# Three sets of transposes moved from the matrix engine to transposing DMAs

## The chip, the cores and the metric

One Trainium2 chip, one core. The metric is the device time of one execution in microseconds (us); lower is better. The core has a matrix engine (PE, with its weight loads listed apart as PEld), a vector engine (DVE), a scalar engine (ACT), GpSimd (POOL) and a synchronising engine (SP) that issues most DMAs. Each engine works through its own list of instructions in order and waits on semaphores for the others.

## The reference

Two independent layers on inputs of 2048 tokens by 448 features, in bfloat16; their outputs are laid side by side.

```
# layer A: a diagonal complex state-space layer, 448 states
Lam_bar = exp(dt * Lam);  B_bar = ((Lam_bar - 1) / Lam)[:, None] * Bmat
Bu = x @ B_bar.T                       # (2048, 448), complex
h[t] = Lam_bar * h[t-1] + Bu[t]        # over 2048 steps
y = 2 * Re(h @ Cmat.T) + x * Dskip
# layer B: 16 heads of 28, each token looks at 8 keys, 2 apart, backwards
q, k, v = split(x @ wqkv)
logits = q . k[pos - 2w] * 28**-0.5,  w = 0..7;  softmax over w
o = sum_w attn[w] * v[pos - 2w];  out = o @ wo
```

## The kernel before

PE multiplies with the contracted axis on the partitions, so both inputs are needed with features on partitions, and so is the attention output `o` before it meets `wo`. Tokens are cut into 16 per partition (token 16p+j is partition p, column j) for the attention output and for layer A, and into four chunks of 512 for the logits. Features are cut 4 by 112. The stages, in program order:

- Loads (SP's queue): layer B's x in four pieces (`xb_sb`), the three parts of `wqkv` (`wqkv_nat`), layer A's `bX` and `cn`, `wo_p`, and later layer A's x (`xa_sb`), which shares its buffer with `xb_sb`.
- Start: PE warm-up matmuls, layer A's parameters (`pt_p`, `pt_d` and many small DVE and ACT operations), then chunk 0 of x transposed (`pt_x`, copied to `xbT`) and projected to kT and qT (`qk_ps`).
- Logit stage, `qk(c)` for four chunks: DVE forms 8 products of q with shifted k (`pr`), PE sums them over features (`lg`); between them PE does the next chunk's transposes and projections, then `setup_b` (`pt_b`, giving `Bcat`) and the v projection (`v_ps`). Each chunk ends in a maximum (`pt_m`, `mx`, `mxb`) and an exponential (`e_all`).
- `norm`: sums of exponentials by PE (`tp`), division by DVE (`rec`, `attn`).
- Value stage, `pv` in four calls of 4 columns: 15 DVE operations each over 128x1792 elements (`pvb`, `pvt`), 60 in all. Each call ends in `tail`: PE transposes `o` (`pt_o`), ACT copies it (`oT`), PE multiplies by `wo_p` (`wo_ps`), ACT copies (`yb`), SP stores.
- Beside it layer A: x transposed (`pt_x`, `xaT`), `local` (`u_ps`, ACT copies `u`) for four column phases b, `scan` over chunks of 16 tokens (`g3`, `rot`, `bak` on PE, `pc`, `psn`, `gsc` on DVE), `groups` (`gt` on PE, `Gt` on DVE), `correct` (`co`) for phases 1, 0 and 2, and `y` per column (`y_ps`, ACT copies `ya`, SP stores).

A scheduler sets each engine's order from the program's order and its own priorities; the order is fixed once built. Every DMA raises one of eight completion semaphores, used in turn, and an issue waits until the DMA that last used its semaphore has landed. PSUM tiles come from three pools by tag: "mm" (3 buffers), "pt" (2), "lg" (3).

Of the kernel before, what the change touches and what calls it, by code (L numbers as in the profile page):

```python
# [31 lines left out]
PL = 64  # L32
MA = 4
# [54 lines left out]
class PartB:  # L88
# [6 lines left out]
    def load_x(self, n0, n1):  # L95
        if n0 == 0:
            self.x_sb = self.pool.tile([NCH, T, D], bf16, name="xb_sb", tag="xin")
        xv = self.B_x[0].rearrange("(n p) d -> p n d", p=NCH)
        self.nc.sync.dma_start(self.x_sb[:, n0:n1, :], xv[:, n0:n1, :])

    def load_w(self, which):
        if which == 1:
            self.wn = self.pool.tile([KP, KT, 3, D], bf16, name="wqkv_nat", tag="wn")
        v = self.B_wqkv.rearrange("(k p) (w c) -> p k w c", p=KP, w=3)
        self.nc.sync.dma_start(self.wn[:, :, which, :], v[:, :, which, :])

    def load_wo(self):
        nc = self.nc
        self.wo_p = self.pool.tile([KP, KT, D], bf16, name="wo_p")
        wo_v = self.B_wo.rearrange("(h kt dl) c -> dl h kt c", kt=KT, dl=7)  # L110
        for dl in range(7):
            nc.sync.dma_start(self.wo_p[dl * H:(dl + 1) * H, :, :], wo_v[dl])

    def alloc(self):
        pool, nc = self.pool, self.nc
        self.xT = pool.tile([KP, KT, S], bf16, name="xbT", tag="xT")
# [35 lines left out]

    def transp(self, n, eng):
        nc, cx = self.nc, self.cx
        pt = cx.ps([KP, KT, 2, NCH], bf16, "pt_x", "pt")
        for i in range(2):
            for k in range(KT):
                nc.tensor.transpose(pt[:, k, i, :], self.x_sb[:, n + i, k * KP:(k + 1) * KP], cx.ident[:])
        cx.ev(eng, self.xT[:, :, n * NCH:(n + 2) * NCH], pt[:].rearrange("p k i c -> p k (i c)"))
# [76 lines left out]
    def pv(self, j0, j1):  # L236
# [16 lines left out]
        for j in range(j0, j1, 2):  # L253
            self.tail(j, acc[:, j - j0:j - j0 + 2])

    def tail(self, j, o_):
        nc, pool, cx = self.nc, self.pool, self.cx
        pt = cx.ps([KP, KT, 2, NCH], bf16, "pt_o", "pt")
        o_ = o_.rearrange("p j d h -> p j (d h)")
        for i in range(2):  # L260
# [3 lines left out]
        nc.scalar.copy(oT[:], pt[:])  # L264
        yb = pool.tile([NCH, 2, D], bf16, name="yb", tag="yb", bufs=2)
        for i in range(2):
            ps = cx.ps([NCH, D], f32, "wo_ps", "lg")
            for kt in range(KT):
                nc.tensor.matmul(ps[:], lhsT=oT[:, kt, i, :], rhs=self.wo_p[:, kt, :], start=(kt == 0),  # L269
                                 stop=(kt == KT - 1))  # L270
            nc.scalar.copy(yb[:, i, :], ps[:])  # L271
        nc.sync.dma_start(self.out_b[:, j:j + 2, :], yb[:])


class PartA:
# [7 lines left out]
    def load_params(self):  # L283
        nc, pool = self.nc, self.pool
        self.prow = pool.tile([3 * NM, 2, PL], bf16, name="prow")
        self.drow = pool.tile([KT, KP], bf16, name="drow")
# [16 lines left out]
    def load_x(self):  # L303
        self.x_sb = self.pool.tile([NCH, T, D], bf16, name="xa_sb", tag="xin")
        xv = self.A_x[0].rearrange("(p j) d -> p j d", j=T)
        for g in range(2):
            self.nc.sync.dma_start(self.x_sb[:, 8 * g:8 * g + 8, :], xv[:, 8 * g:8 * g + 8, :])
# [10 lines left out]
    def params(self):  # L318
# [79 lines left out]
    def params_g(self):  # L398
# [46 lines left out]
    def setup_b(self, engs):  # L445
        nc, cx, pool = self.nc, self.cx, self.pool
        self.Bcat = pool.tile([KP, KT, NM, NCH], bf16, name="Bcat")
        for i in range(NM):
            pt = cx.ps([KP, KT, NCH], f32, "pt_b", "pt")
            for k in range(KT):  # L450
                nc.tensor.matmul(pt[:, k, :], lhsT=self.bX[:, i, k * KP:(k + 1) * KP], rhs=self.mats["g"][:, i, :],
                                 start=(k == 0), stop=(k == KT - 1), skip_group_check=True)
            cx.ev(engs[i % len(engs)], self.Bcat[:, :, i, :], pt[:])
            yield
# [14 lines left out]
    def alloc(self):  # L469
        pool = self.pool  # L470
        xa = pool.tile([KP, 4, KT, 4, NCH], bf16, name="xaT", tag="xT")
        self.xT = {i: xa[:, i] for i in range(4)}
        u01 = pool.tile([NCH, 2, NM, 4 * NCH], bf16, name="u01", tag="q")
        self.h = [u01[:, 0], u01[:, 1], None, None]

    def transp(self, b, eng):
        nc, cx = self.nc, self.cx
        t_ = self.xT[b]
        for a in range(0, 4, 2):
            pt = cx.ps([KP, KT, 2, NCH], bf16, "pt_x", "pt")  # L480
            for i in range(2):
                for k in range(KT):
                    nc.tensor.transpose(pt[:, k, i, :], self.x_sb[:, 4 * (a + i) + b, k * KP:(k + 1) * KP],
                                        cx.ident[:])
            cx.ev(eng, t_[:, :, a:a + 2, :], pt[:])
            yield

    def local(self, b):
        nc, cx = self.nc, self.cx
        if b == 2:  # L490
            u23 = self.pool.tile([NCH, 2, NM, 4 * NCH], bf16, name="u23", tag="xin")
            self.h[2], self.h[3] = u23[:, 0], u23[:, 1]
        for m in range(NM):
            ps = cx.ps([NCH, 4 * NCH], f32, "u_ps", "mm")
            for k in range(KT):
                nc.tensor.matmul(ps[:], lhsT=self.Bcat[:, k, m, :], rhs=self.xT[b][:, k].rearrange("p a c -> p (a c)"),  # L496
                                 start=(k == 0), stop=(b % 2 == 0 and k == KT - 1))
            if b % 2:
                nc.tensor.matmul(ps[:], lhsT=self.mats[1][:, m, :], rhs=self.h[b - 1][:, m, :], start=False,
                                 stop=(b == 1))  # L500
            if b == 3:
                nc.tensor.matmul(ps[:], lhsT=self.mats[2][:, m, :], rhs=self.h[1][:, m, :], start=False, stop=True)  # L502
            nc.scalar.copy(self.h[b][:, m, :], ps[:])  # L503
# [7 lines left out]
    def scan(self):  # L511
# [6 lines left out]
        pc = [pool.tile(tab, bf16, name=f"pc{i}") for i in range(2)]  # L518
        psn = [pool.tile(tab, bf16, name=f"psn{i}") for i in range(2)]
        g = pool.tile(tab, f32, name="gsc")  # L520
# [78 lines left out]
    def y(self, a, b):  # L599
# [3 lines left out]
        for k in range(KT):  # L603
            nc.tensor.matmul(ps[:, k * KP:(k + 1) * KP], lhsT=self.xT[b][:, k, a, :], rhs=self.Dg[:, k, :],  # L604
# [10 lines left out]
def body(ctx: ExitStack, tc: tile.TileContext, A_x, A_Lre, A_Lim, A_Bre, A_Bim, A_Cre, A_Cim, A_logdt, A_Dskip,  # L615
# [54 lines left out]
    for _ in chain(transp(0), proj(0), transp(1)):  # L670
        pass
    weave(b.qk(0), chain(proj(1), transp(2)), 2)
    weave(b.qk(1), chain(proj(2), transp(3)), 2)
    a.params_g()
    weave(b.qk(2), chain(proj(3), a.setup_b("A")), 2)
    a.load_x()
# [4 lines left out]
    for _ in a.transp(0, "A"):  # L681
        pass
    weave(a.local(0), chain(a.transp(1, "A"), a.transp(2, "A")))
    weave(a.local(1), chain(a.transp(3, "A"), a.setup_c("A")))
    for b_ in (2, 3):
# [8 lines left out]
    for b_ in (1, 0, 2):  # L694
        for _ in a.correct(b_, "A"):
# [39 lines left out]
```

## Time and profile before

| | |
|---|---|
| Time, median of 2 runs | 178.68 us (177.88 to 179.47) |
| The profiled execution: time | 177.29 us |
| The profiled execution: span of the trace | 175.3 us |
| PE busy | 159.6 us |
| DVE busy | 132.6 us |
| ACT busy | 108.9 us |
| POOL busy | 5.6 us |

The profiled execution took 1.99 us more than its span, for what lies before the first and after the last traced instruction. Rows of the timeline read: start, length, engine, line, operation, output<-input, sizes, count, and in brackets how long the engine was idle before it and what ended that. SPq is SP's queue issuing DMAs.

### The profile page before, as it was taken

The page shows a single profiled execution, that of the slowest core. Times are in us where ns is not written, and L with a number is a line of the kernel's source. Part 1 is how long each engine was busy: PE and PEld are TensorE (multiplying, and loading weights), DVE is VectorE, ACT ScalarE, POOL GpSimd, SP SyncE. Part 2 cuts the span into 40 slices and gives each one's busy share as a digit, 9 for nine tenths or more (in the row PEclk, how much of TensorE's full clock was granted, in tenths as well). Part 3 has the DMA queues.
Part 4 walks back from the last instruction along what each step waited for, and adds up shares of the span by engine and source line. Part 5 has one row for each costly group of instructions (what it writes and reads, how often), then busy time and mean ns, then how long its engine had stood idle before and what let it go on. Part 6 is the DMA issues. An engine that isn't in the chain of part 4 may idle for free.

```text
span 175.3 us, 2965 instructions
## 1 busy us (share of the span) xinstructions
PE 159.6 (91%) x1171; PEld 90.8 (52%) x1175; DVE 132.6 (76%) x189; ACT 108.9 (62%) x183; POOL 5.6 (3%) x37
## 2 busy tenths in 40 slices
PE   7589798799799999999999999969999999999981
PEld 4355333445444766676565444746755455554550
DVE  1299998999996894039999999999999999900000
ACT  2279444775744876788899654356238739738382
POOL 8400000000000000000000000000000000000000
PEclk9999999999999999999999999999999999999999
DMA  5999851000370004170000000002111230140113
GB/s 155 291 297 179 90 119 30 0 4 0 87 332 0 6 0 109 50 200 8 0 4 0 0 0 0 4 0 77 33 52 52 79 108 26 52 132 30 52 54 105
DMA packets 16589, 12.36 MB, mean 70 GB/s; under 512 B 7219, under 2 KB 16065, under 8 KB 16575
## 3 DMA queue, kind: packets, MB, share of 16 engines
q1 hardware_dynamic: 16504, 12.16, 26.2%
q8 instruction: 9, 0.15, 0.4%
q14 instruction: 5, 0.04, 0.1%
q10 hardware_dynamic: 71, 0.01, 0.0%
HBM read 6.89 MB, written 3.67 MB: 60 GB/s over the span
## 4 chain that ended last, share of the span: by engine, by line
PE 51%; DVE 32%; ACT 10%; DMA 3%; issue 1%; ACTq 1%
PE y_ps L607 11%; PE qk_ps L165 11%; DVE pvb L252 9%; DVE pvt L249 8%; PE v_ps L177 7%; PE wo_ps L269 5%; PE lg L196 5%; DVE pr L192 4%; DMA drow<-in_A_Dskip_dram 3%; PE co L577 2%; ACT u L588 2%; DVE pvb L249 2%; PE y_ps L604 2%; ACT oT L264 2%; PE gt L566 1%
## 5 line engine op out<-in xcount | busy, mean ns | idle before, releaser
L192 DVE TENSOR_TENSOR pr<-qT,kT 112x2048 bf16<-112x2048 bf16 x32 | 37.0, 1219 | 0.5 <-ACT qT L77 0.5
L165 PE MATMUL qk_ps<-xbT,wqkv_nat 112*112 112x512 bf16 x128 | 32.3, 386 | 1.4 <-ACT xbT L77 1.1
L252 DVE TENSOR_TENSOR pvb<-pvb,pvt 128x1792 bf16<-128x1792 bf16 x28 | 30.3, 1083 | 0.0
L249 DVE TENSOR_TENSOR pvt<-attn,vd 128x1792 bf16<-128x1792 bf16 x28 | 30.0, 1083 | 0.0
L496 PE MATMUL u_ps<-xaT,Bcat 112*128 112x512 bf16 x112 | 27.4, 379 | 0.1
L503 ACT CAST u<-u_ps 128x512 bf16<-128x512 f32 x28 | 16.5, 590 | 9.2 <-PE u_ps L502 5.0
L165 PEld LDWEIGHTS <-wqkv_nat 112*112 112x112 bf16 x128 | 14.9, 129 | 14.1 <-issue 6.9
L607 PE MATMUL y_ps<-C,u 128*128 128x448 bf16 x84 | 18.0, 352 | 0.0
L610 ACT CAST ya<-y_ps 128x448 bf16<-128x448 f32 x16 | 8.5, 533 | 15.1 <-PE y_ps L607 14.2
L496 PEld LDWEIGHTS <-Bcat 112*128 112x128 bf16 x112 | 10.5, 97 | 10.8 <-issue 0.2
L269 PE MATMUL wo_ps<-wo_p,oT 112*128 112x448 bf16 x64 | 14.3, 353 | 1.0 <-ACT oT L264 0.9
L196 PE MATMUL lg<-pr,onesW 112*32 112x512 bf16 x128 | 12.8, 387 | 1.1 <-DVE pr L192 1.1
L177 PE MATMUL v_ps<-wqkv_nat,xbT 112*128 112x448 bf16 x64 | 13.7, 357 | 0.0
L77 ACT CAST kT<-qk_ps 112x512 bf16<-112x512 f32 x14 | 8.2, 584 | 8.1 <-PE qk_ps L165 8.1
L77 ACT CAST qT<-qk_ps 112x512 bf16<-112x512 f32 x14 | 8.2, 584 | 6.7 <-PE qk_ps L165 6.7
L271 ACT CAST yb<-wo_ps 128x448 bf16<-128x448 f32 x16 | 8.6, 539 | 5.8 <-PE wo_ps L269 5.6
L77 ACT CAST vd<-v_ps 128x448 bf16<-128x448 f32 x16 | 8.5, 533 | 4.5 <-PE v_ps L177 4.3
L177 PEld LDWEIGHTS <-xbT 112*128 112x128 bf16 x64 | 8.8, 146 | 4.0 <-issue 1.3
L210 DVE TENSOR_REDUCE mx<-pt_m 128x64 bf16<-128x512 bf16 x4 | 2.7, 687 | 10.5 <-PE pt_m L209 10.5
L588 ACT CAST u<-co 128x512 bf16<-128x512 f32 x21 | 10.6, 629 | 0.0
L607 PEld LDWEIGHTS <-u 128*128 128x128 bf16 x84 | 7.6, 97 | 5.5
L264 ACT COPY oT<-pt_o 112x1024 bf16<-112x1024 bf16 x8 | 8.1, 1047 | 2.5 <-PE pt_o L262 2.5
(175 smaller groups left out, 218.5 us busy)
## 6 DMA issues: line engine op xcount, KB each, us to landing
xb_sb<-in_B_x_dram SPq DMA_DIRECT2D x4, 448.0 KB, 7.0
xa_sb<-in_A_x_dram SPq DMA_DIRECT2D x2, 896.0 KB, 6.4
out_dram<-yb SPq DMA_DIRECT2D x8, 224.0 KB, 2.1
out_dram<-ya SPq DMA_DIRECT2D x16, 112.0 KB, 1.7
wqkv_nat<-in_B_wqkv_dram SPq DMA_DIRECT2D x3, 392.0 KB, 6.4
vd<-vd SPq DMA_DIRECT2D x1, 784.0 KB, 5.3
vd<-vd SPq DMA_DIRECT2D x1, 588.0 KB, 4.3
bX<-in_A_B_re_dram SPq DMA_DIRECT2D x1, 392.0 KB
```

Source lines behind the costliest of these rows:

```text
L77: nc.scalar.copy(out, in_)
L165: nc.tensor.matmul(ps[:], lhsT=self.wn[:, k, which, g * KP:(g + 1) * KP], rhs=self.xT[:, k, c * CH:(c + 1) * CH], start=(k == 0), stop=(k ...
L177: nc.tensor.matmul(ps[:], lhsT=xv[:, k, j, :], rhs=self.wn[:, k, 2, :], start=(k == 0), stop=(k == KT - 1))
L192: V.tensor_tensor(pr[:], self.qT[:, :, c * CH:(c + 1) * CH], self.kT[:, :, k0:k0 + CH], op=ALU.mult)
L196: nc.tensor.matmul(lg[NW * g:NW * (g + 1), :], lhsT=self.onesW[:, NW - 4 - 4 * w:2 * NW - 4 - 4 * w], rhs=pr[:, g, :], start=(w == 0), sto ...
L249: V.tensor_tensor(t_[:, 0:n], self.at[:, w, j0:j1, :].unsqueeze(2).to_broadcast([NCH, n, DH, H]), self.vd[:, off:off + n], op=ALU.mult)
L252: V.tensor_tensor(acc[:, 0:n], acc[:, 0:n], t_[:, 0:n], op=ALU.add)
L269: nc.tensor.matmul(ps[:], lhsT=oT[:, kt, i, :], rhs=self.wo_p[:, kt, :], start=(kt == 0), stop=(kt == KT - 1))
L496: nc.tensor.matmul(ps[:], lhsT=self.Bcat[:, k, m, :], rhs=self.xT[b][:, k].rearrange("p a c -> p (a c)"), start=(k == 0), stop=(b % 2 == 0 ...
L503: nc.scalar.copy(self.h[b][:, m, :], ps[:])
L588: nc.scalar.copy(h_, ps[:])
L607: nc.tensor.matmul(ps[:], lhsT=self.state(m, a, b), rhs=self.C[:, m, :], start=False, stop=(m == NM - 1), skip_group_check=True)
```

## The change

All 192 PE transposes named `pt_x` and `pt_o`, and the copies behind them, are gone. In their place stand 13 transposing DMAs on SP's queue.

- Layer B's x: each chunk of 512 tokens is written transposed into `xbT` by two DMAs from HBM, one for features 0 to 383 (three slabs of 128), one for features 320 to 447. `wqkv` is loaded in the same cut; the fourth slab's first 64 rows are zero (a memset on POOL), since those features are in the third slab already. Each part of `wqkv` is two DMAs.
- Layer A's x: one DMA turns 128 partitions by 7168 values into 56 slabs of 128x128 (`xaT`). Two tokens are 896 values, seven slabs; the even token uses slabs 0 to 3, the odd one 3 to 6, and the shared slab 3 is half one token's and half the other's. So `Bcat` exists in two versions (56 `pt_b` matmuls where there were 28, 14 evictions where there were 7, alternately ACT and DVE) with zeroed halves, and `Dg` has seven blocks. The load is issued with the others at the start; it no longer waits for `xb_sb`.
- The attention output: `tail` runs once per `pv` call, and one DMA turns 128x1792 values of `o` from SBUF to SBUF into 14 slabs (`oT`). `wo_p` is laid out to match, with 24 small DMAs where there were 7.
- `correct(2)`: the matmul with the identity and ACT's copy become an addition by DVE (7 of them). `setup_c` moves beside `local(0)`.

```diff
+    def load_x(self, c):
+        if c == 0:
+            self.xT = self.pool.tile([NCH, KT, S], bf16, name="xbT", tag="xT")
+        sl = slice(c * CH, (c + 1) * CH)
+        x_ = self.B_x[0][sl, :]
+        self.nc.sync.dma_start_transpose(out=self.xT[:, 0:3, sl], in_=x_[:, 0:3 * NCH])
+        self.nc.sync.dma_start_transpose(out=self.xT[:, 3, sl], in_=x_[:, D - NCH:D])
...
-        for dl in range(7):
-            nc.sync.dma_start(self.wo_p[dl * H:(dl + 1) * H, :, :], wo_v[dl])
+        for g in range(8):
+            p = slice(g * H, (g + 1) * H)
+            nc.sync.dma_start(self.wo_p[p, 0:3, :], kv(g))
+            nc.sync.dma_start(self.wo_p[p, 5:8, :], kv(4 + g))
+            nc.sync.dma_start(self.wo_p[p, 3 + g // 4, :], wo_v[24 + g if g < 4 else g - 4])
...
-        for j in range(j0, j1, 2):
-            self.tail(j, acc[:, j - j0:j - j0 + 2])
+        self.tail(j0, acc)
+    def tail(self, j0, o_):
...
-            for kt in range(KT):
-                nc.tensor.transpose(pt[:, kt, i, :], o_[:, i, kt * KP:(kt + 1) * KP], cx.ident[:])
-        oT = pool.tile([KP, KT, 2, NCH], bf16, name="oT", tag="oT", bufs=2)
-        nc.scalar.copy(oT[:], pt[:])
+        oT = pool.tile([NCH, 2 * NSL, NCH], bf16, name="oT", tag="oT", bufs=2)
+        nc.sync.dma_start_transpose(out=oT[:], in_=o_.rearrange("p j d h -> p (j d h)"))
...
     def load_x(self):
-        for g in range(2):
-            self.nc.sync.dma_start(self.x_sb[:, 8 * g:8 * g + 8, :], xv[:, 8 * g:8 * g + 8, :])
+        self.xs = self.pool.tile([NCH, NSL * T // 2, NCH], bf16, name="xaT", tag="xin")
+        self.nc.sync.dma_start_transpose(out=self.xs[:], in_=self.A_x[0].rearrange("(p j) d -> p (j d)", j=T))
...
-    weave(b.qk(2), chain(proj(3), a.setup_b("A")), 2)
-    a.load_x()
+    weave(b.qk(2), chain(proj(3), a.setup_b("AV")), 2)
...
-        for _ in a.correct(b_, "A"):
+        for _ in a.correct(b_, "V" if b_ == 2 else "A"):
```

The order changes at three places that matter below. First, SP's queue at the program's start, with the semaphores that an issue waits for. Before:

```order
L99 DMA xb_sb<-in_B_x_dram 128x4x448
L105 DMA wqkv_nat<-in_B_wqkv_dram 112x4x448 x2
L99 DMA xb_sb<-in_B_x_dram 128x4x448
L99 DMA xb_sb<-in_B_x_dram 128x4x448 [waits DMAHW0_49]
L99 DMA xb_sb<-in_B_x_dram 128x4x448 [waits DMAHW1_49]
```

Of the change, at the same place:

```order
L102 DMA_TRANSPOSE xbT<-in_B_x_dram 128x3x512
L103 DMA_TRANSPOSE xbT<-in_B_x_dram 128x512
L110 DMA wqkv_nat<-in_B_wqkv_dram 128x3x448
L111 DMA wqkv_nat<-in_B_wqkv_dram 64x448 [waits DMAHW1_49]
L110 DMA wqkv_nat<-in_B_wqkv_dram 128x3x448 [waits DMAHW3_49]
L111 DMA wqkv_nat<-in_B_wqkv_dram 64x448 [waits DMAHW4_49]
L102 DMA_TRANSPOSE xbT<-in_B_x_dram 128x3x512 [waits DMAHW5_49]
```

DMAHW1 and DMAHW4 are the semaphores of the first two transposing DMAs, so the last rows of the k weights, the q weights and chunk 1 are issued only once chunk 0 has landed transposed; all of it now stands behind it in SP's order.

Second, PE's list at the end of the logit stage (`lg` is the last chunk's sum, `pt_m` the transposes for its maximum; weight loads between). Before, `pt_m` follows the last v projection and layer A's transposes come behind it:

```order
L177 MATMUL v_ps<-wqkv_nat,xbT 128x448
L209 LDWEIGHTS lgb
L209 MATMUL pt_m<-ident,lgb 128x128
```

Of the change:

```order
L199 MATMUL lg_816<-pr,onesW 32x512
L491 LDWEIGHTS Bcat
L491 MATMUL u_ps<-xaT,Bcat 128x512
L491 LDWEIGHTS Bcat
L491 MATMUL u_ps<-xaT,Bcat 128x512
L491 LDWEIGHTS Bcat
L491 MATMUL u_ps<-xaT,Bcat 128x512
L491 LDWEIGHTS Bcat
L491 MATMUL u_ps<-xaT,Bcat 128x512
L212 LDWEIGHTS lgb
L212 MATMUL pt_m<-ident,lgb 128x128
```

Four matmuls of `local(0)`, which read layer A's transposed x, now stand ahead of `pt_m`.

Third, the end of DVE's list. Before, it is the last `pv` call's products and sums alone, ending so:

```order
L249 TENSOR_TENSOR pvt_1479<-attn,vd 128x1792
L252 TENSOR_TENSOR pvb<-pvb,pvt_1478 128x1792
L249 TENSOR_TENSOR pvt_1480<-attn,vd 128x1792
L252 TENSOR_TENSOR pvb<-pvb,pvt_1479 128x1792
L252 TENSOR_TENSOR pvb<-pvb,pvt_1480 128x1792
```

Of the change:

```order
L252 TENSOR_TENSOR pvt_1392<-attn,vd 128x1792
L255 TENSOR_TENSOR pvb<-pvb,pvt_1391 128x1792
L252 TENSOR_TENSOR pvt_1393<-attn,vd 128x1792
L585 TENSOR_TENSOR u_1029<-co,u_1029 128x512 x7
L255 TENSOR_TENSOR pvb<-pvb,pvt_1392 128x1792
L255 TENSOR_TENSOR pvb<-pvb,pvt_1393 128x1792
```

The seven additions of `correct(2)` stand ahead of the last two sums, so the last `oT` waits for them. Further up in DVE's list, 24 of the 60 `pv` operations stand ahead of the scan's first one, where 32 did.

More of the change, by code (lines that the diff above doesn't have):

```diff
@@ L151, in zero_halo @@
                                self.cx.wz[0:1, 0:D].unsqueeze(1).to_broadcast([1, HALO, D]))
[L153 to L159, printed above, removed]
     def proj_t(self, c, g, which, eng):
@@ L446, in setup_b @@
         nc, cx, pool = self.nc, self.cx, self.pool
-        self.Bcat = pool.tile([KP, KT, NM, NCH], bf16, name="Bcat")
+        self.Bcat = pool.tile([NCH, 2, KT, NM, NCH], bf16, name="Bcat")
         for i in range(NM):
[L449 to L454, printed above, removed]
+            for v in range(2):
+                pt = cx.ps([NCH, KT, NCH], f32, "pt_b", "pt")
+                for k in range(KT):
+                    d0 = SLAB[3 * v + k]
+                    nc.tensor.matmul(pt[:, k, :], lhsT=self.bX[:, i, d0:d0 + NCH], rhs=self.mats["g"][:, i, :],
+                                     start=(k == 0), stop=(k == KT - 1), skip_group_check=True)
+                cx.ev(engs[(2 * i + v) % len(engs)], self.Bcat[:, v, :, i, :], pt[:])
+                yield
+        nc.gpsimd.memset(self.Bcat[PL:NCH, 0, 3], 0.0)
+        nc.gpsimd.memset(self.Bcat[0:PL, 1, 0], 0.0)
     def setup_c(self, engs):
@@ L469, in alloc @@
     def alloc(self):
[L470 to L486, printed above, removed]
+        u01 = self.pool.tile([NCH, 2, NM, 4 * NCH], bf16, name="u01", tag="q")
@@ L517, in scan @@
         tab = [NCH, NM, NCH]
-        pc = [pool.tile(tab, bf16, name=f"pc{i}") for i in range(2)]
-        psn = [pool.tile(tab, bf16, name=f"psn{i}") for i in range(2)]
-        g = pool.tile(tab, f32, name="gsc")
+        rt = pool.tile([NCH, 4, NM, NCH], bf16, name="rt", tag="Bcat")
+        pc, psn = (rt[:, 0], rt[:, 1]), (rt[:, 2], rt[:, 3])
+        g = pool.tile(tab, f32, name="gsc", tag="cn")
         self.Hc = pool.tile([NCH, NM, 2 + NCH], bf16, name="Hc")
@@ L680, in body @@
     a.alloc()
[L681 to L685, printed above, removed]
+    weave(a.local(0), a.setup_c("A"))
+    for b_ in (1, 2, 3):
         for _ in a.local(b_):
```

116 lines of the change are left out of this document (61 added, 55 removed).

## The prediction

> **What bounds the kernel now.** I read the busy times first, then the slices, then the timeline of each engine for what ended its idle time.
>
> ```profile
> PE 159.6 (91%) x1171; PEld 90.8 (52%) x1175; DVE 132.6 (76%) x189; ACT 108.9 (62%) x183; POOL 5.6 (3%) x37
> PE   7589798799799999999999999969999999999981
> DVE  1299998999996894039999999999999999900000
> DMA  5999851000370004170000000002111230140113
> ```
>
> PE is the bound by the busy times, and the slices say how: DVE has holes at a third and at 45% of the span and is empty in the last five slices, while PE has hardly any. So PE's backlog sets two stages, the logit stage up to 75 us and the tail after 153 us; between them DVE is as full as PE. The DMA engines are mostly free from slice 8 on.
>
> ```profile
> 57.84 0.69 DVE L210 TENSOR_REDUCE mx<-pt_m 128x64 bf16<-128x512 bf16 x1 [2.51 <-PE pt_m L209]
> 75.78 0.69 DVE L210 TENSOR_REDUCE mx<-pt_m 128x64 bf16<-128x512 bf16 x1 [7.97 <-PE pt_m L209]
> 82.72 1.08 DVE L249 TENSOR_TENSOR pvb<-attn,vd 128x1792 bf16<-128x1792 bf16 x1
> 83.72 2.09 DVE L249 TENSOR_TENSOR pvt<-attn,vd 128x1792 bf16<-128x1792 bf16 x2
> 150.97 2.21 DVE L252 TENSOR_TENSOR pvb<-pvb,pvt 128x1792 bf16<-128x1792 bf16 x2
> 168.38 3.20 PE L269 MATMUL wo_ps<-wo_p,oT 112*128 112x448 bf16 x16 [0.69 <-ACT oT L264]
> ```
>
> DVE waited 7.97 us for PE's v projections before the last maximum. From 82.72 it ran the 60 `pv` operations at 1.0 us each (83.72 less 82.72) and the scan's, and was done at 153.2; PE needed 18.4 us more. After PE's last matmul at 171.6 come one copy and the store: 3.7 us to the end of the span.
>
> **What is removed, and its price.** A transpose's own length overstates it, so I take start to start:
>
> ```profile
> 80.96 0.61 PE L483 MATMUL pt_x<-ident,xa_sb 128*112 128x128 bf16 x8
> 81.41 0.38 PE L496 MATMUL u_ps<-xaT,Bcat 112*128 112x512 bf16 x1
> 132.10 0.38 PE L577 MATMUL co<-u,ident 128*128 128x512 bf16 x1
> 132.31 0.22 PE L584 MATMUL co<-Hc,mat 128*128 128x128 bf16 x1
> L83 DVE CAST kT<-qk_ps 112x512 bf16<-112x512 f32 x2 | 1.4, 692 | 0.3 <-PE qk_ps L165 0.3
> ```
>
> Eight transposes take 0.45 us, 0.056 each; 192 are 10.8 us. The seven identity matmuls of `correct(2)` are 0.21 each, 1.5 us. 28 more `pt_b` cost 1.6 us. PE falls by 10.7, to about 149. DVE gains seven additions and seven `Bcat` evictions of 128x512 values from PSUM, each at most the 0.69 of the cast (0.62 start to start), 4.3 us for each seven, and loses one `xbT` copy: about 140.6. ACT loses some 24 copies of 1 us; I cost that at nothing, since ACT is 62% busy and off the end's chain. POOL's five new memsets are on an idle engine. So PE and DVE come out nearly level, and no sum of busy times gives the end; I follow the stages.
>
> **Start.**
>
> ```profile
> DMA to landing us min/median/max: 4.0/7.0/7.9
> 9.45 0.65 PE L158 MATMUL pt_x<-ident,xb_sb 128*112 128x128 bf16 x8 [1.67 <-DVE kf L354]
> 16.48 1.02 PE L165 MATMUL qk_ps<-xbT,wqkv_nat 112*112 112x512 bf16 x4 [0.34 <-ACT qT L77]
> 19.06 0.81 PE L165 MATMUL qk_ps<-xbT,wqkv_nat 112*112 112x512 bf16 x3 [1.10 <-ACT xbT L77]
> 45.09 0.61 PE L158 MATMUL pt_x<-ident,xb_sb 128*112 128x128 bf16 x8 [0.73 <-DVE mx L210]
> ```
>
> The first row is `xb_sb`'s: chunk 0 (448 KB) landed 4.0 us after its issue at 0.8. A transposing DMA isn't in this trace; at plain speed chunk 0 is there at 4.8, and what waits for it (last k rows, q weights) some 3 us later, at 8. The 16 q matmuls at 0.25 each, plus 2 us for evictions, end chunk 0's projections at 14 where they ended at 17.5: 3.5 us won.
>
> ```profile
> 18.56 9.17 DVE L192 TENSOR_TENSOR pr<-qT,kT 112x2048 bf16<-112x2048 bf16 x8
> 54.24 1.09 DVE L437 TENSOR_TENSOR mat<-Dm,Scat 128x896 bf16<-128x896 f32 x1
> 75.36 0.39 PE L209 MATMUL pt_m<-ident,lgb 128*128 128x128 bf16 x4
> ```
>
> Up to the last `pt_m`, at 75.4, PE also loses the 40 transposes that came after chunk 0's projections (2.25 us) and the two waits 1.10 and 0.73; it gains 1.6 of `pt_b` and 0.9 of the four `u_ps` set ahead. 75.4 - 3.5 - 2.25 - 1.8 + 1.6 + 0.9 = 70.3. DVE would be ready sooner: the first product at some 15.5, 32 of them at 1.15 (36.7), 2.5 of parameter work that now stands behind the first, three maxima at 0.9, 2.3 for `matg` and small operations, 4.3 for `Bcat` make 64. So PE still decides.
>
> **From the last maximum to the scan.** From `pt_m` to the first `pv` it took 7.4 us; DVE now has `mat4` in that chain (1.0, the row at 54.24), and `mat8`, `mat12` in a gap 0.4 too short: 8.8, so `pv` starts at 79.1. 24 operations later, at 103.2, DVE reaches the scan.
>
> ```profile
> 113.08 0.33 PE L529 MATMUL g3B<-u,mat 128*128 128x128 bf16 x3
> 114.78 0.68 DVE L531 TENSOR_TENSOR pc<-g3A,cosE 128x512 bf16<-128x512 f32 x1
> 126.00 0.36 PE L604 MATMUL y_ps<-Dg,xaT 112*128 112x112 bf16 x4
> 126.45 0.56 DVE L568 TENSOR_TENSOR Gt<-gt,u 128x384 bf16<-128x384 f32 x1 [0.27 <-issue]
> 135.32 0.54 PE L269 MATMUL wo_ps<-wo_p,oT 112*128 112x448 bf16 x2
> ```
>
> PE needed 37.9 us from `pt_m` to its last `g3`; without 64 transposes (3.6), a 0.34 wait and the four matmuls set ahead it is 33, so it ends at 103.3. Both arrive together, 11.4 us earlier than before. Scan and groups keep their 12.2 us: last `Gt` at 115.5, first `y` matmul at 114.5.
>
> **The end.** Here the new wait decides: a `tail` can't start until its DMA has landed. Call that L. Nearest rows:
>
> ```profile
> 0.80 0.44 SPq L99 DMA_DIRECT2D xb_sb<-in_B_x_dram  x1
> vd<-vd SPq DMA_DIRECT2D x1, 784.0 KB, 5.3
> vd<-vd SPq DMA_DIRECT2D x1, 588.0 KB, 4.3
> 9.04 8.56 SPq L301 DMA_DIRECT2D cn<-in_A_C_re_dram  x4
> 17.64 4.23 SPq L301 DMA_DIRECT2D cn<-in_A_C_im_dram  x4
> 21.92 4.46 SPq L112 DMA_DIRECT2D wo_p<-in_B_wo_dram  x7
> ```
>
> The two SBUF-to-SBUF copies differ by 196 KB and 1.0 us: 196 GB/s and 1.3 us fixed, so 448 KB of `o` takes 3.6 at least. The loads of `cn`, in runs of 128 bytes, were paced at 46 and 93 GB/s (392 KB in 8.56 and 4.23 us); at 93, L is 6.1. L is a wait, so it can't be a gain by itself. I take 5, between the copy's 3.6 and 6.1, and keep both.
>
> PE's order after 114.5: four `y` (6.1 us, from 126.00 to 132.10 before) and a `correct` (3.2, to 135.32 before) to 123.8. The second `pv` call ends five operations after `Gt`, 120.5, its DMA at 125.5: PE waits 1.7. `wo_ps` 3.2, `y` 6.1, `correct` 3.2, one `y` 1.5: 139.5. The third call ends at 135.5, lands at 140.5: 1.0 of waiting; `wo_ps` and three `y`: 148.3. DVE, twelve operations on at 147.6, then adds `correct(2)`'s seven results (4.4): 153. PE's last four `y` end at 159.1; DVE's last two sums end at 155, their DMA at 160. Then `wo_ps` 3.2 and 3.7 to the end: span 166.9, against 175.3. With the 1.99 around the span that is **169 us** against this execution's 177.29; the median of the runs shown, 178.68, lies 0.8% above that, which the range covers. With L at 3.6 the same chain gives 167, at 6.1 it gives 171; past 5 a microsecond of L costs about two, as three of the DMAs are waited for in turn. Queued behind each on SP are stores of `ya` (two buffers), which ACT waits for; I cost that at nothing, because the store behind the second call's DMA is of the fourth `y`, and its buffer is written again only after `wo_ps` and two more `y`, 11 us later.
>
> The Trainium skill, "Advanced Engine Details and Errata", section "X-Bar Transpose (TRN2)", says that transposing DMAs run as fast as plain ones, at 350 to 400 GB/s. No run here shows it; by that, as an estimate, L is near 2.5 and the sum 167, the same as with 3.6.
>
> **Rivals.** *Late layer-A input: slower.* Four `u_ps` ahead of the last `pt_m` read `xaT`, so if it lands after 69.4, PE and then DVE stop for the difference. SP's queue had issued everything but `xa_sb` by 26.4; with 17 more `wo_p` loads at 0.64 (10.9) and nine other issues more at 0.5 (the first row's 0.44), `xaT` is issued at 41.8 at plain speed. It and layer B's x are 3.94 MB transposed; at a rate r, `xaT` lands at 35.9 plus 3.94 MB/r (the 35.9 takes off the 7.2 us that layer B's x takes at the 290 GB/s of the first slices).
>
> ```profile
> GB/s 155 291 297 179 90 119 30 0 4 0 87 332 0 6 0 109 50 200 8 0 4 0 0 0 0 4 0 77 33 52 52 79 108 26 52 132 30 52 54 105
> ```
>
> At 196 that is 56, hidden; from 118 GB/s down it is late. At `cn`'s 93 it is 9 us late, and with L at 6.1 the time is 180. At `cn`'s 46 it is 52 late and L 11: about 233. It is slower than before by 2% from some 88 GB/s down. For it: transposing reads runs of 256 bytes, nearer to `cn`'s 128 than to the long runs of `xb_sb`. Against it: `cn` was loaded behind other traffic.
>
> The Trainium skill, "VectorE: DVE Perf Modes", section "The three transpose paths", gives 1309 ns for a 128x128 block by DMA and 390 ns by TensorE. No run here shows whether blocks overlap. If they didn't, that is 25 GB/s, and the estimate by this page is about 320 us; I count it into this rival.
>
> *A slow SBUF-to-SBUF transpose: no change.* With HBM's in time but L of 8, the chain of the end gives 175; at 11 it gives 180. For it: an SBUF-to-SBUF transpose reads 128 partitions in pieces where `vd` moved long runs. Against it: nothing else of size moves in that stage, by the DMA slices.
>
> **Chances.** Forecast, transposes at 118 GB/s or more and L under 8: 0.60, times 163 (L of 3.6 and PE's remaining 2 to 4 us of waits in the logit stage gone) to 174. No change, by L of 8 to 11 or a rate of 88 to 118: 0.14. Late `xaT` below 88 GB/s: 0.26. A difference under 2% is what a measurement of this kernel can't tell from none, so these are also the chances of faster, same and slower. The range is 163 to 193: it takes in the forecast, the middle case and late `xaT` down to about 67 GB/s.
>
> **What would show it.** First `pr` product near 15 to 16 us; the last `pt_m` near 70; DVE's wait before its `mx` gone or under 3 us; the first `pc` near 103; the `oT` DMAs 4 to 6 us to landing; the end's chain through `pvb`, the `oT` DMA and `wo_ps`. It is wrong if `u_ps` or its weight loads wait for `xaT`, if chunk 0's first `qk_ps` starts after 9, or if `wo_ps` waits over 3 us for a DMA more than once.

## The result: 167.6 us, and the profile after

The changed kernel took 167.57 us (two runs, 167.32 and 167.82) against 178.68: a ratio of 0.938, with a 95% interval of 0.919 to 0.957. Run again later, beside other kernels, it gave 0.940 (0.934 to 0.947). Some executions, of the kernel before above all, took one to four per cent longer than the fastest of their kernel; medians further on include them, ratios don't.

The profiled execution after took 167.32 us, its span is 165.6. First the page's busy times and slices, which answer to the four lines shown of before.

```profile
PE 150.5 (91%) x1002; PEld 79.6 (48%) x1004; DVE 140.1 (85%) x202; ACT 84.7 (51%) x156; POOL 9.4 (6%) x42
PE   6599899999999999999999999859999997988870
DVE  1069999999799679989999999999999999999100
DMA  4699896533890500240000050030171316320633
```

PE fell by 9.1 us, DVE rose by 7.5, ACT fell by 24. The holes of DVE at a third and at 45% of the span have shrunk, and of its five empty slices at the end two are left. DVE is now busy until nearly the end.

Two windows of the logit stage, from the first product to the start of the last `pt_m`, show what the busy times hide. Columns: stretch, its length, then busy time and instructions of PE, PE's weight loads, DVE, ACT and POOL, the granted clock, DMA share and GB/s; the first row is of before, the second of after.

```profile
18.56:75.36 56.80, 53.19 (x374) 28.13 (x373) 46.14 (x55) 35.01 (x59) 0.00 (x0) 1.00 0.23 62
```

```profile
16.81:70.73 53.92, 53.20 (x366) 26.65 (x366) 50.08 (x70) 32.24 (x57) 1.68 (x2) 1.00 0.52 111
```

TensorE's work in this stage is the same, 53.2 us, since 28 more `pt_b` and four `u_ps` stand where the transposes stood. Its idle time fell from 3.6 to 0.7 us: layer B's transposes had cost TensorE not only their own length but waiting as well.

Now the timeline after, at the places that the prediction named.

```profile
7.22 2.15 PE L168 MATMUL qk_ps<-xbT,wqkv_nat 128*112 128x512 bf16 x9 [1.71 <-DMA wqkv_nat<-in_B_wqkv_dram]
16.81 1.22 DVE L195 TENSOR_TENSOR pr<-qT,kT 112x2048 bf16<-112x2048 bf16 x1
69.85 1.04 PE L491 MATMUL u_ps<-xaT,Bcat 128*128 128x512 bf16 x4
70.73 0.39 PE L212 MATMUL pt_m<-ident,lgb 128*128 128x128 bf16 x4
71.15 0.69 DVE L213 TENSOR_REDUCE mx<-pt_m 128x64 bf16<-128x512 bf16 x1 [0.42 <-PE pt_m L212]
79.43 1.08 DVE L252 TENSOR_TENSOR pvb<-attn,vd 128x1792 bf16<-128x1792 bf16 x1
103.48 0.68 DVE L526 TENSOR_TENSOR rt<-g3A,cosE 128x512 bf16<-128x512 f32 x1
114.39 0.36 PE L602 MATMUL y_ps<-Dg,xaT 128*128 128x64 bf16 x4
124.30 3.20 PE L267 MATMUL wo_ps<-wo_p,oT 128*128 128x448 bf16 x16 [0.45 <-DMA oT<-pvb]
139.36 3.20 PE L267 MATMUL wo_ps<-wo_p,oT 128*128 128x448 bf16 x16 [0.98 <-DMA oT<-pvb]
147.37 4.28 DVE L585 TENSOR_TENSOR u<-co,u 128x512 bf16<-128x512 f32 x7
151.57 2.21 DVE L255 TENSOR_TENSOR pvb<-pvb,pvt 128x1792 bf16<-128x1792 bf16 x2
158.28 3.20 PE L267 MATMUL wo_ps<-wo_p,oT 128*128 128x448 bf16 x16 [1.53 <-DMA oT<-pvb]
```

DVE's wait of 7.97 us before the last maximum is 0.42; the scan starts 11.3 us earlier than in before, and the end of the span comes 9.7 us earlier. So 1.6 us were given back between the scan and the end. The brackets show a new loss there: `wo_ps` waits three times for a landing.

The chain that ended last (start, length, what) shows the same from behind, and the list of waits the sum (engine, line, waited for: total, times, longest).

```profile
120.30 3.95 DMA oT<-pvb
135.36 3.95 DMA oT<-pvb
153.84 4.39 DMA oT<-pvb
```

```profile
PE wo_ps L267 <- DMA oT<-pvb: 3.0, 3, 1.5
```

### The profile page after: what moved, and what is told of

It is laid out like the page before. It is cut to its first block, busy times and chain, and to the rows that moved or that the text cites. A ratio compares the mean times of both kernels' runs of the same rounds, so it can differ in the third digit from the quotient of the medians.

```text
span 165.6 us, 2656 instructions
## 1 busy us (share of the span) xinstructions
PE 150.5 (91%) x1002; PEld 79.6 (48%) x1004; DVE 140.1 (85%) x202; ACT 84.7 (51%) x156; POOL 9.4 (6%) x42
## 4 chain that ended last, share of the span: by engine, by line
PE 53%; DVE 24%; DMA 9%; ACT 6%; issue 3%; SPq 2%; DVEq 0%
PE qk_ps L168 16%; DVE pvb L255 8%; PE v_ps L180 8%; DVE pvt L252 8%; DMA oT<-pvb 7%; PE y_ps L605 7%; PE lg L199 7%; PE wo_ps L267 6%; PE u_ps L491 2%; DMA wqkv_nat<-in_B_wqkv_dram 2%; DVE u L585 2%; PE pt_b L459 2%; DVE pvb L252 2%; DVE gsc L535 1%; DVE Gt L563 1%
## 5 line engine op out<-in xcount | busy, mean ns | idle before, releaser
L168 PE MATMUL qk_ps<-xbT,wqkv_nat 128*112 128x512 bf16 x128 | 32.4, 386 | 2.1 <-DMA wqkv_nat<-in_B_wqkv_dram 1.7
L491 PE MATMUL u_ps<-xaT,Bcat 128*128 128x512 bf16 x112 | 27.7, 379 | 0.1
L168 PEld LDWEIGHTS <-wqkv_nat 128*112 128x112 bf16 x128 | 14.9, 129 | 14.2 <-issue 4.8
L267 PE MATMUL wo_ps<-wo_p,oT 128*128 128x448 bf16 x64 | 13.5, 353 | 3.0 <-DMA oT<-pvb 3.0
L491 PEld LDWEIGHTS <-Bcat 128*128 128x128 bf16 x112 | 10.6, 98 | 11.5 <-issue 0.2
L180 PE MATMUL v_ps<-wqkv_nat,xbT 128*128 128x448 bf16 x64 | 15.9, 363 | 0.0
L267 PEld LDWEIGHTS <-oT 128*128 128x128 bf16 x64 | 5.9, 98 | 9.5 <-DMA oT<-pvb 4.1
L180 PEld LDWEIGHTS <-xbT 128*128 128x128 bf16 x64 | 8.1, 147 | 4.0 <-issue 2.5
L199 PEld LDWEIGHTS <-onesW 112*32 112x32 bf16 x128 | 3.7, 92 | 11.4 <-issue 10.7
L583 ACT CAST u<-co 128x512 bf16<-128x512 f32 x14 | 7.1, 629 | 0.0
```

The lines of the kernel that those rows point to most:

```text
L168: nc.tensor.matmul(ps[:], lhsT=self.wn[:, k, which, g * KP:(g + 1) * KP], rhs=self.xT[:, k, c * CH:(c + 1) * CH], start=(k == 0), stop=(k ...
L180: nc.tensor.matmul(ps[:], lhsT=xv[:, k, j, :], rhs=self.wn[:, k, 2, :], start=(k == 0), stop=(k == KT - 1))
L199: nc.tensor.matmul(lg[NW * g:NW * (g + 1), :], lhsT=self.onesW[:, NW - 4 - 4 * w:2 * NW - 4 - 4 * w], rhs=pr[:, g, :], start=(w == 0), sto ...
L267: nc.tensor.matmul(ps[:], lhsT=oT[:, NSL * (j // 2) + 3 * (j % 2) + k, :], rhs=self.wo_p[:, KT * (j % 2) + k, :], start=(k == 0), stop=(k ...
L491: nc.tensor.matmul(ps4[:], lhsT=self.Bcat[:, b % 2, k, m, :], rhs=self.xs[:, s0::2 * NSL, :], start=(k == 0), stop=(b % 2 == 0 and k == KT ...
```

## The experiments

Theory after the result: both inputs bring TensorE time and remove its waits up to the scan; the output's DMA removes 3.6 us of TensorE work, and its landing is a new wait at the end. The main rival: the output too brings a real share of the gain.

**The output by TensorE again.** The kernel after with the `load_wo` and `tail` of before:

```diff
-        nc.sync.dma_start_transpose(out=oT[:], in_=o_.rearrange("p j d h -> p (j d h)"))
+                nc.tensor.transpose(pt[:, kt, i, :], o_[:, i, kt * KP:(kt + 1) * KP], cx.ident[:])
...
+        nc.scalar.copy(oT[:], pt[:])
```

> The kernel after, with only the attention output turned by TensorE again (64 transposes, ACT evictions, the old layout of the output weights). Theory (the DMA of the output buys TensorE time, its landing costs waits): TensorE gets 64 x 0.056 = 3.6 us back and some 0.35 us of waiting for ACT per token pair, and loses the three waits for oT (0.45 + 0.98 + 1.53 = 3.0 us); net 1 to 3 us slower than after, some 168.5 to 170.5. Rival (waits for landing cost more than the transposes they replace): faster than after, 165 or less. Second rival (the whole gain of the change is in the output): 175 or more.

Measured: 166.75 us, ratio 0.938 (0.932 to 0.943). It isn't slower, so the theory missed by some 2 us, towards the first rival, whose 165 it doesn't reach. The page and the groups (busy, mean ns, idle before) show both halves of the exchange:

```profile
PE 154.6 (94%) x1066; PEld 83.6 (51%) x1068; DVE 140.0 (85%) x202; ACT 92.0 (56%) x164; POOL 8.5 (5%) x40
L261 ACT COPY oT<-pt_o 112x1024 bf16<-112x1024 bf16 x8 | 7.9, 1053 | 4.5 <-PE pt_o L259 4.5
```

TensorE works 4.1 us more and ACT 7.3 us more in a span 0.6 us shorter. What the output's DMA saves, TensorE spends idle at the end, 3.0 us of it in the three waits. In this kernel the scheduler also sets the last `pv` ahead of the seven additions of `correct(2)`, so that it ends at 149.3 and not at 153.8. That order counts by itself: the run with `correct(2)` on ACT, further on, keeps the output's DMA, ends the last `pv` at 150.0 and took 166.18 us. Held against that run, this one is 0.6 us slower with intervals that overlap. So beside the inputs the output's DMA is worth some half a microsecond or nothing.

**The output alone by DMA.** The kernel before with the `load_wo` and `tail` of after; for room, the scan's tables share the tiles that they share in after.

```diff
-        for j in range(j0, j1, 2):
-            self.tail(j, acc[:, j - j0:j - j0 + 2])
+        self.tail(j0, acc)
```

> The kernel before, with only the attention output turned by DMA (and the output weights laid out for it); both x inputs are still turned by TensorE. Theory: in before TensorE is the one that is late at the end (its last wo_ps starts 15 us behind the end of the last pv), so the landing times are hidden and the 64 transposes (3.6 us) and 0.7 us of waiting for ACT go: 4 us faster than before, some 174.5. Rival (landing is waited for here too): no change, 177 to 179. Rival (whole gain in the output): 168 to 170.

Measured: 177.15 us, the median of four runs from 174.14 to 178.35, too far apart to tell. So it was run again.

> The kernel before with only the attention output turned by DMA, again, since two of the first four runs had a lower clock than the runs beside them. If landing is hidden there: 174 to 175; if the wait that the first trace shows (1.0 us for oT, behind it the evictions of y) is typical: 176 to 177.

Measured: 177.01 us, ratio 0.976 (0.964 to 0.989). The same edit that shows no gain in after is worth some 4 us in before, 2 to 6 by the interval. There TensorE is far behind DVE at the end, so a landing is mostly hidden and the transposes count in full; one wait of 1.0 us stood in the first run's trace:

```profile
144.24 0.36 PE L271 MATMUL wo_ps<-wo_p,oT 128*128 128x448 bf16 x1 [1.04 <-DMA oT<-pvb]
```

**Layer A's input by TensorE.**

```diff
-        self.nc.sync.dma_start_transpose(out=self.xs[:], in_=...)
+                nc.tensor.transpose(pt[:, i, :], self.xn[:, (s0 + i) * NCH:(s0 + i + 1) * NCH], cx.ident[:])
+            cx.ev(eng, self.xs[:, s0:s0 + 8, :], pt[:])
```

> The kernel after, with layer A's x loaded plainly and turned by 56 TensorE transposes in seven groups of eight, into the same slabs of 128 (ACT evicts them), ahead of the first u_ps. Theory (the gain of the inputs is TensorE time ahead of the scan, where TensorE and DVE arrive together): 56 x 0.056 = 3.1 us more for TensorE there, some 0.4 us of waiting for an eviction; scan 3 to 3.5 us later, 170.5 to 171. Rival (TensorE has room there, layer B's input brings all): 167 to 168.

Measured: 172.70 us, ratio 0.971 (0.964 to 0.979). More than the 3.5 expected. These transposes stand alone between `pt_m` and the first `u_ps`, and for room their slabs take the place of `xbT` (the tile's view: count, least, median and most ns, first and last start):

```profile
L320 PE MATMUL pt_x<-ident,xa_sb x56: 216/219/219, 70.8 to 77.5; 128*128 128x128 bf16 x56
77.65 1.02 PE L505 MATMUL u_ps<-xaT,Bcat 128*128 128x512 bf16 x4
```

`u_ps` starts 7.8 us later than after's 69.85: not 56 times 0.056, but the pace of ACT's evictions, seven copies of 1.02 us, with some maximum and softmax work of TensorE between them. The last `g3` starts at 109.2, 6.1 us later. What follows isn't the transposes alone: at 116.5 a `wo_ps` waits 2.04 us for `oT`, and eight others from 118.2 on take 3.07 us where eight took 1.68 in the repeat of after, at a granted clock of 0.50 between 118 and 120 us.

**Layer B's input by TensorE.** Its 64 transposes, woven into the projections as in before, into the slabs of after; layer A's load moves behind `b.qk(2)`.

```diff
-        self.nc.sync.dma_start_transpose(out=self.xT[:, 0:3, sl], in_=x_[:, 0:3 * NCH])
+                nc.tensor.transpose(pt[:, k, i, :], self.x_sb[:, n + i, d0:d0 + NCH], cx.ident[:])
+        cx.ev(eng, self.xT[:, :, n * NCH:(n + 2) * NCH], pt[:].rearrange("p k i c -> p k (i c)"))
```

> The kernel after, with layer B's x loaded plainly and turned by 64 TensorE transposes into the same slabs of 128 (evicted by ACT, for the first chunk by ACT and DVE); layer A's x is loaded later, when the room of layer B's is free. Theory: 3.6 us more TensorE time and some 2 us of waits for evictions ahead of the last pt_m, less up to 1 us from weights that are issued sooner: pv and scan 4 to 5 us later, 171.5 to 173. Rival (layer A's x brings all): 167 to 168. The two runs with one input each should add up to about the 11 us between before and after, since the output alone brought nothing.

Measured: 178.82 us, ratio 1.007 (1.003 to 1.011). All of the gain is gone, twice what was expected. Rows of its timeline, and windows:

```profile
10.37 0.62 PE L110 MATMUL pt_x<-ident,xb_sb 128*128 128x128 bf16 x8 [3.00 <-DVE kf L368]
12.00:14.00 2.00, 2.00 (x6) 1.06 (x5) 0.00 (x0) 1.66 (x7) 0.00 (x0) 0.50 1.12 318
21.72 1.22 DVE L203 TENSOR_TENSOR pr<-qT,kT 112x2048 bf16<-112x2048 bf16 x1
81.26 0.69 DVE L221 TENSOR_REDUCE mx<-pt_m 128x64 bf16<-128x512 bf16 x1 [5.06 <-PE pt_m L220]
21.72:80.83 59.11, 55.39 (x401) 29.10 (x401) 50.99 (x67) 34.65 (x59) 1.68 (x2) 1.00 0.29 63
164.00:166.00 2.00, 2.00 (x10) 1.06 (x9) 0.12 (x1) 0.53 (x1) 0.00 (x0) 0.50 0.00 0
```

Of the 10.1 us by which the last maximum is late, 4.9 are there at the first product. From there to the last `pt_m` it took 59.1 us against 53.9 in after: TensorE worked 2.2 us more and stood still 3.0 us more. It is later even than before's 75.78, so the kernel isn't "before with layer A's DMA": it has before's transposes and after's 28 more `pt_b`.

It also runs at a lower clock. Behind the wait of 3.00 us, for an eviction that stands behind parameter work on DVE, the granted clock was 0.50 from 12 to 14 us, and chunk 0's 32 `qk_ps` took 8.83 us (32 took 7.24 in after). Near the end, behind a wait of 1.84 us for `oT`, it was 0.50 to 0.52 from 162 to 168 us, and two `y` took 4.8 us where two took 3.0 in after. All ten runs have a mean clock of 0.966 to 0.979; in after all but one lie between 0.987 and 1.0. So by these two rows, as an estimate, some 3.4 of the 11 us are the clock (1.6 and 1.8).

The two losses, 5 and 11 us, don't add up to 11 either. From after, each input turned by TensorE costs more than its share; how much of the rest of layer B's loss is the 28 `pt_b` and the later load of layer A's x, these runs don't separate.

**Every landing doubled.**

```diff
-        nc.sync.dma_start_transpose(out=oT[:], in_=o_...
+        for _ in range(2): nc.sync.dma_start_transpose(out=oT[:], in_=o_...
```

> The kernel after, with every oT DMA issued twice in a row into the same tile, so that the tile is landed some 8 us behind pv instead of 4; the scheduler moves one y ahead of two of the wo_ps groups for it. Theory (the landing is waited for in turn, two us for each us of landing): 5 to 8 us slower than after, 173 to 176. Rival (only the last landing counts, the other two are covered by other TensorE work): 4 us, 171 to 172.

Measured: 176.56 us, ratio 0.992 (0.987 to 0.997), 9 us slower than after, above the 5 to 8 expected. The waits and what follows them:

```profile
PE wo_ps L267 <- DMA oT<-pvb: 9.0, 3, 5.5
128.79 4.82 PE L267 MATMUL wo_ps<-wo_p,oT 128*128 128x448 bf16 x16 [2.26 <-DMA oT<-pvb]
146.11 3.20 PE L267 MATMUL wo_ps<-wo_p,oT 128*128 128x448 bf16 x16 [1.25 <-DMA oT<-pvb]
165.94 5.01 PE L267 MATMUL wo_ps<-wo_p,oT 128*128 128x448 bf16 x16 [5.48 <-DMA oT<-pvb]
129.00:134.00 5.00, 5.00 (x22) 2.26 (x21) 5.00 (x6) 1.95 (x4) 0.00 (x0) 0.69 0.11 39
166.00:171.00 5.00, 4.95 (x16) 1.92 (x16) 0.00 (x0) 1.61 (x4) 0.00 (x0) 0.63 0.08 27
```

Six us more of waiting, and 1.6 and 1.8 us more for the same sixteen matmuls after the long waits, at a granted clock of 0.69 and 0.63: together 9.4, against 9.3 between the spans. The first wait grew by 1.8 us, the second by 0.3, the last by 4.0. So the rival, that only the last counts, falls, though the last brings most; the second was nearly hidden.

**`correct(2)` back to ACT.** A small edit inside the change, a term of DVE's end in the prediction.

```diff
-        for _ in a.correct(b_, "V" if b_ == 2 else "A"):
+        for _ in a.correct(b_, "A"):
```

> The kernel after, with the results of correct(2) added by TensorE and evicted by ACT, as before, instead of added by DVE. In after's trace DVE spends 4.28 us on these seven additions, in the midst of the last pv, and ACT idles 4.54 us meanwhile; the last oT DMA starts when that pv ends. Theory (DVE and the landing end the kernel): the last pv ends 4.3 us sooner, oT lands before TensorE's last y matmul is done, so wo_ps starts when those end, 1.5 to 2 us sooner: 165.5 to 166. Rival (TensorE ends it; seven more matmuls at 0.22 us are on its path): 1.5 us slower, 169.

Measured: 166.18 us, ratio 0.934 (0.929 to 0.939); the intervals of the two ratios overlap a little, the span is 164.1 against 165.6.

```profile
147.80 2.21 DVE L255 TENSOR_TENSOR pvb<-pvb,pvt 128x1792 bf16<-128x1792 bf16 x2
156.86 3.19 PE L267 MATMUL wo_ps<-wo_p,oT 128*128 128x448 bf16 x16
```

The last `pv` ends 3.8 us sooner, and the last `wo_ps` starts 1.4 us sooner with no wait in brackets: TensorE ends the kernel here, DVE and the landing ended it in after. By these traces the seven additions on DVE cost 1.4 us; they weren't free.

**The start.** Two tries to get the first weights sooner.

```diff
+    b.load_w(1)
     b.load_x(0)
-    b.load_w(1)
```

> The kernel after, with the first weight load (wqkv_nat for k) issued ahead of the two transposing DMAs of layer B's first chunk. In after these two take 1.36 and 1.61 us to issue, the weights are issued at 3.88 and the first qk_ps starts at 7.22. Theory (issue time of the transposing DMAs on SP delays the start): first qk_ps at some 6, everything up to the last pt_m 1.2 us sooner, 166 to 166.6. Rival (DVE's parameter work, done at 16.7, or the transposing DMAs that now land 1.3 us later set the start): no change, 167.3 to 168.

Measured: 167.04 us, ratio 0.940 (0.935 to 0.945): no difference from after that these runs can tell. The wait only changes its name:

```profile
6.88 2.10 PE L168 MATMUL qk_ps<-xbT,wqkv_nat 128*112 128x512 bf16 x9 [1.37 <-DMA xbT<-in_B_x_dram]
```

The second try had ACT's queue load the first weights, on top of the edit of `correct(2)`:

```diff
+    b.load_x(0)
+    b.load_w(1, nc.scalar)
     a.load_params()
-    b.load_x(0)
-    b.load_w(1)
```

> The kernel of the experiment that gives correct(2) back to ACT, and the first weight load issued on ACT's DMA queue beside the transposing DMAs on SP, instead of behind or ahead of them. Theory: weights and the first three slabs land at about 4.5 to 5.5, the fourth slab near 6.7, so the first qk_ps starts 1 to 1.5 us sooner and all that follows with it: 164.7 to 165.2. Rival (the fourth slab's landing sets the start): 0.4 us sooner, 165.8.

Measured: 168.35 us, ratio 0.949 (0.943 to 0.955), 2 us slower than without it. The first `qk_ps` does start at 6.3, but ACT's loads of `drow`, behind the weights, are issued at 6.0 to 7.9 and not from 2.1, and TensorE's ninth matmul is followed by the small transposes of `prow` and `drow`, from which DVE's parameter work starts. The first product starts at 18.56, 1.75 us later than in after:

```profile
11.08 0.16 PE L339 MATMUL pt_d<-ident,drow 7*128 7x7 bf16 x1 [2.37 <-DMA drow<-in_A_Dskip_dram]
```

**Layer A's load twice,** the margin of the prediction's slower rival:

```diff
-        self.nc.sync.dma_start_transpose(out=self.xs[:], ...
+        for _ in range(2): self.nc.sync.dma_start_transpose(out=self.xs[:], ...
```

> The kernel after, with layer A's transposing DMA issued twice in a row into the same tile; the rest stands in the same order. In after it is issued at 40.9, lands at 50.2, and is first needed at 69.9. Theory (20 us to spare): landed near 60, SP busy 7.3 us longer, no wait of TensorE for xaT: the time of after within 0.5 us. Rival (margin is smaller than it looks, since the copies of vd stand behind it on SP): 2 us slower or more.

Measured: 168.21 us, ratio 0.945 (0.937 to 0.953); after, on the same chip, has 0.940 (0.934 to 0.947). SP's queue issues both, the second once the first has landed:

```profile
40.09 7.03 SPq L310 DMA_TRANSPOSE xaT<-in_A_x_dram  x1
49.17 6.95 SPq L310 DMA_TRANSPOSE xaT<-in_A_x_dram  x1
69.97 1.04 PE L491 MATMUL u_ps<-xaT,Bcat 128*128 128x512 bf16 x4
```

`u_ps` starts at 69.97 without a wait, so a transfer at half the rate would be hidden as well. The difference of 0.9 us in the medians isn't explained by a wait, and the intervals overlap.

**After again, and a faster version.** The first of these two is the reference for the second, on one chip.

> The kernel after, unchanged, on the same chip as the three runs beside it, so that they can be held against it: 167 to 168, ratio to before 0.935 to 0.945.

Measured: 167.34 us, ratio 0.940 (0.934 to 0.947).

```diff
+    b.load_w(1)
     b.load_x(0)
-    b.load_w(1)
...
-        for _ in a.correct(b_, "V" if b_ == 2 else "A"):
+        for _ in a.correct(b_, "A"):
...
+        a.y(0, b_)
         if b_ == 1:
             b.pv(4, 8)
...
-        for a_ in range(4):
+        for a_ in range(1, 4):
```

> The kernel after with three edits: correct(2) by TensorE and ACT, the first weight load ahead of the first transposing DMAs, and in each round of the end the first y ahead of the wo_ps group that waits for a landing. Theory (TensorE is busy from its start to the end but for the waits for oT, 0.54 and 0.67 us in the run with correct(2) by ACT): these go, with the 0.4 us of the earlier start and the 1.4 us that correct(2) brought: 2.5 to 3 us faster than after on the same chip, 164.5 to 165. Rival (the waits come back as waits for ACT or for the out stores): 1.5 to 2 us faster, 165.5 to 166.

Measured: 165.04 us, ratio 0.928 (0.921 to 0.934). Its six runs lie between 164.5 and 165.5, those of after beside them between 166.9 and 167.7 but for one of 169.9, so it beats both kernels.

```profile
125.34 3.19 PE L267 MATMUL wo_ps<-wo_p,oT 128*128 128x448 bf16 x16
133.92 0.53 ACT L608 CAST ya<-y_ps 128x448 bf16<-128x448 f32 x1 [1.73 <-DMA out_dram<-ya]
134.51 0.38 PE L572 MATMUL co<-u,ident 128*128 128x512 bf16 x1 [0.54 <-ACT ya L608]
139.46 3.20 PE L267 MATMUL wo_ps<-wo_p,oT 128*128 128x448 bf16 x16 [0.82 <-DMA oT<-pvb]
```

The first wait for `oT` is gone; the second stays, because its DMA starts no sooner than `pv` allows. In its place ACT waits at 133.9 for stores that are queued on SP, and TensorE half a microsecond for ACT.

## Why the prediction was right, step by step

The forecast was 169, the runs gave 167.3 to 167.8.

| Step | predicted | after |
|---|---|---|
| first product `pr` | 15.5 | 16.81 |
| last `pt_m` | 70.3 | 70.73 |
| DVE's wait before the last maximum | under 3 | 0.42 |
| first `pv` | 79.1 | 79.43 |
| DVE reaches the scan | 103.2 | 103.48 |
| landing of `oT`, L | 5 | 3.95, 3.95, 4.39 |
| waits of `wo_ps` for it | 1.7, 1.0, 1 | 0.45, 0.98, 1.53 |
| DVE's last sums | 155 | 153.8 |
| last `wo_ps` | 160 | 158.28 |
| span | 166.9 | 165.6 |

**The start** was mis-sized by 1.3 us. The sum had the q matmuls begin at 8, when the q weights are there. In fact TensorE waited for the k weights until 7.22, and the 16 k matmuls had to come first: 12 of them by 10.3, the q matmuls from some 11.4 to 15.1, where the sum had 14. Then DVE's own list decided: the small transposes that its parameter work waits for stand behind nine `qk_ps`, at 9.3 (6.2 in before), and from 10.11 to the first product at 16.81 DVE had no gap. SP's queue needs 1.36 and 1.61 us to issue the two transposing DMAs ahead of the weights, where the prediction took the row of a plain one, 0.44:

```profile
0.81 1.36 SPq L102 DMA_TRANSPOSE xbT<-in_B_x_dram  x1
2.22 1.61 SPq L103 DMA_TRANSPOSE xbT<-in_B_x_dram  x1
3.88 0.58 SPq L110 DMA_DIRECT2D wqkv_nat<-in_B_wqkv_dram  x1
10.53 7.24 PE L168 MATMUL qk_ps<-xbT,wqkv_nat 128*112 128x512 bf16 x32 [0.24 <-ACT kT L79]
```

**The logit stage** made up for most of it: from the first product to the last `pt_m` it took 53.9 us where the sum had 54.8. The sum took off two waits, 1.10 and 0.73; the windows show 2.9 us of standing idle removed. That the two errors nearly cancel, so that the last `pt_m` is right to 0.4 us, is luck.

**The middle** held within 0.3 us, and so did the reasoning that TensorE and DVE reach the scan together. The run with layer A's input by TensorE shows that transposes set alone there cost more than their length, as evictions pace them.

**The end** held in its form, three landings waited for in turn, and its main term was 1 us too large: L is 3.95, between the 3.6 of the lower bound and the 5 taken. That is the 1.3 us by which the forecast was high: with 3.95 the prediction's own chain puts the last `wo_ps` at 158.2 (158.28 measured) and the end of the span at 165.1; what follows that `wo_ps` took 7.3 us, not 6.9, and gave some of it back. The slope of two us for each us of L doesn't hold for long landings: four us more gave 6.0 of waiting and 3.4 from the clock, in an order that one `y` had changed; without the clock that is 1.5 for each. The stores of `ya`, put at nothing, made ACT wait 5.8 us in three pieces, and TensorE 0.23 for ACT: the term was rightly left out.

**The rivals.** *Late layer-A input* turned on a rate below 118 GB/s. `xaT` is 56 blocks of 32 KiB, 1.84 MB, and landed 9.3 us after its issue, 197 GB/s, near the 196 of the `vd` copies that the sum had used; it was there at 50.2, 19.6 us before its use. *A slow SBUF-to-SBUF transpose* with L at 8 was priced at 175; the run with doubled landings made it 176.6. Its mechanism is real, its condition wasn't met.

**What the prediction didn't say** is which part brings the gain. It summed three parts, each right in its place, and the chain showed new waits where the output's transposes had been. The runs settle the split: both inputs alone give 166.75, all that the change gives; the output gives some 4 us on its own, and beside the inputs half a microsecond or nothing. The seven additions on DVE stood in its chain of the end at 4.4 us; the run without them gained 1.4, since TensorE is ready only that much sooner.

**Two rules of the Trainium skill,** cited in the prediction. "Advanced Engine Details and Errata", section "X-Bar Transpose (TRN2)", has transposing DMAs as fast as plain ones at 350 to 400 GB/s. These traces differ: 197 GB/s for the largest, landing included, 9.3 us where the plain load of the same bytes in before had landed 6.9 us after its first issue. From `oT`'s 14 blocks in 3.95 us and `xaT`'s 56 in 9.3 one gets, as an estimate across two sources (SBUF and HBM), 2.2 us fixed and 0.127 us for a block, about 257 GB/s. "VectorE: DVE Perf Modes", section "The three transpose paths", gives 1309 ns for a block. Set against it, the same estimate has some ten blocks overlap in one DMA, so the 320 us, worked out as if none did, was far off.

## What to carry to other kernels

In these runs a transpose that moved from TensorE to a DMA brought its start-to-start time, and the waits for its evictions, where TensorE was behind and the data needed late; where another engine's result is turned at the end of a chain, the landing (4 us here) took back what TensorE saved. Two parts of a change that ease the same engine don't add, so run each part alone, in both directions. When an engine becomes nearly level with the bound, look for small pieces given to it in the same change: the seven additions here cost 1.4 us, and giving them back, with one `y` of each round set ahead of a wait and the first weights issued first, brought 2.3 us.

## What the runs showed that was not expected

SP is held for long by a transposing DMA: 1.3 to 1.7 us for four or 12 blocks from HBM, 1.5 to 2.0 for 14 from SBUF, and 7.25 us for the 56 of `xaT`, where one plain load of weights takes 0.4 to 0.7:

```profile
40.92 7.25 SPq L310 DMA_TRANSPOSE xaT<-in_A_x_dram  x1
xaT<-in_A_x_dram SPq DMA_TRANSPOSE x1, 9.3
```

What stands behind it on that queue waits: the weights at the start, and at the end stores of `ya`, for which ACT waited 5.8 us in all. How much of these 5.8 us is the held queue wasn't tested.

A wait of TensorE of 2.3 us, in the run with doubled landings, was followed by five us at a mean clock of 0.69, of which 130 to 132 us show 0.50; waits of up to 1.53 us in the trace of after left `wo_ps` at its 3.20 us. The Trainium skill, "TensorE: Matmul & The Clock Gate", section "Part 1: The HAM clock gate", puts the drop to half clock behind an idle window of some 3.4 us. The 0.50 agrees with its half clock, but here it came after a shorter wait, and the measurement decides. Nor is it the length of one wait that decides: in both traces of after TensorE waits 1.54 us at about 109, in four us of which it works two; in the first the clock stays at 1.00, in the repeat it is 0.85 in these four us and 0.72 in the next four. What tells the two apart, these runs don't show.

```profile
112.00:116.00 4.00, 3.90 (x39) 2.77 (x39) 4.00 (x9) 0.04 (x1) 0.00 (x0) 1.00 0.02 6
112.00:116.00 4.00, 4.00 (x35) 3.24 (x35) 3.58 (x8) 0.00 (x0) 0.00 (x0) 0.72 0.01 4
```

The first row is of after, the second of its repeat.
